# Weight sums of the first pair spread over VectorE and GpSimd, conversions moved behind the gate product, one weight quarter kept in DRAM until it is needed

## The chip, the core and the metric

The kernel runs on one core of a Trainium2 chip. A core has TensorE (PE in the profile, with its weight loads as PEld), VectorE (DVE), ScalarE (ACT), GpSimd (POOL) and SyncE (SP, which here only issues DMAs). Each engine works through its own queue of instructions in order and waits on semaphores for what the others made. The metric is the device time of one execution in microseconds, the median of several runs. The profile is one further execution, and its span is a little shorter than the timed runs.

## The reference

The program is a cross-attention between tokens and a small state, for 8 batches and 8 heads, and a feed-forward block over the joined result (cut to what matters):

```python
# x: (8, 8, 512, 64)   state: (8, 8, 32, 64)   scale = 1/8
a     = softmax(scale * x @ state.T)        # 512 x 32 for each batch and head
xread = a @ state                           # 512 x 64
a2    = softmax(scale * state @ x.T)        # 32 x 512
sread = a2 @ x                              # 32 x 64
y = concat([xread, sread], axis=2)          # 544 rows for each batch and head
y = y.transpose(0, 2, 1, 3).reshape(8 * 544, 512)
h = y @ w_in                                # 512 -> 2048
g = h * cos(h)
out = g @ w_out                             # 2048 -> 512
```

All activations are 32-bit floats. The two weight matrices, `w_in` and `w_out`, arrive as 64-bit floats; the kernel itself turns them into 32-bit ones.

## The kernel before, in words

**Tiles and steps.** The work is a list of tiles. A tile is 128 of the 2048 hidden columns of one batch: PE makes `h` for the batch's 512 tokens in PSUM (`hidden`, L490), then the gate turns it into `g` in four instructions that alternate between ACT and DVE:

- `gate`, ACT L560: rounds `h` to a whole number of turns
- `gate2`, DVE L563: subtracts, which leaves the fraction
- `gate3`, ACT L566: the sine of it, shifted, which is the cosine
- `gate4`, DVE L580: the product with `h`, written to `g_all`

One tile is one step: 16 steps for each of 8 batches, then 16 for the states. Batches are taken in pairs, 32 steps each (`PERIOD`). In the first pair (`first_pair`, steps 0 to 27, and the first four steps of the general schedule, `later_pair`, 28 to 31) two tiles of `h` are in flight, in two PSUM banks. From the second pair on, two tiles are gated in one instruction (128x1024). The main loop at the end of the program emits, step after step, the instructions of every engine in a fixed order. What comes earlier in the loop stands earlier in an engine's queue. A list for each step (`stage_at`, `sums_at`, `outer_at`, `weights_at`) says what is added in it beside the gate. The steps of attention for the next batch are put in by `plan`, as lists by engine (`go(0)` is PE, `go(1)`, `go(2)` and `go(5)` ACT, `go(3)` and `go(4)` DVE).

**Attention is folded in.** The product of states and `w_in` is made once for each batch (`products`, kept in `sw`), so that `h` needs a depth of 256 (8 heads of 32 states) in place of 512.

**The second product saves multiplications.** `out = g @ w_out` is done for a pair of batches as a two-by-two block product with 7 instead of 8 multiplications (Winograd's form): `p1` to `p7`, each with a weight block of its own, a sum or difference of the quarters `a11`, `a12`, `a21`, `a22` of `w_out`. Each of the seven is done in the same way once more inside (`Product`, 7 stages of 8 PE instructions each, L745). The sums of `g` that these need are made by DVE (`outer_sum`, L692) and POOL (`sums`, L692). From batch 2 on, three quarters of the `h` tiles are also done with 7 blocks: `seven_part` on PE (L540), `sw_sums` on POOL for the weights (L523, into `swS_all`), and `halves` on DVE for the attention side (L509, into `aS_all`). Only for batch 0 of the first pair are `p1` and `p2` done plainly, tile after tile, beside the gate (`first_product` in steps 4 to 11, `second_product` in odd steps 13 to 27, L633), with `a11` and `a12`.

**The weights are prepared in the first pair.** They are loaded raw as 18 blocks (1 MB for most), into three buffers, `raw_at`. `convert(i, parts)` turns block i into 32-bit floats: parts "1" and "2" are on ACT (L243, L246; "2" leaves its part in `low`, which is the memory of `aS_all`), "b" and "c" on DVE (L249, L252), "d" on POOL (L257), and "f" issues the load of a later block into the freed buffer. `conv_at` names the block of a step: blocks 4 to 12 in steps 0 to 8, blocks 13 to 17 in steps 11 to 15. ACT does "1" and "2" in that step; DVE and POOL do their parts in the next one, between `gate2` and `gate4`.

Then the seven weight blocks of `p1` to `p7` are made by `weight_sum` (L1092: outer sums over a whole quarter) and, for each of the seven, `inner_weights` (L671: four sums on POOL into a buffer of temporaries `TEMPS`, then eight stores to the DRAM tensor `blocks_kept`). Before, this runs in steps 16 to 25 on POOL, except for two of the outer sums, on DVE. Only `a12`'s block waits until step 50 (`last_weights`). During the pairs, `fetch_block` brings the blocks back, three stages ahead, through a ring of 4 buffers. All these DMAs are issued by SP, in order.

**Memory is tight.** `g_all` has 12 buffers of four tiles ("quads"). The list `quads_free` hands them out, oldest first, to `gate4`, to `sums`, and for temporaries; a11, a12, a21, a22 and SQ (a21+a22) occupy quads 5, 6, 7, 8 and 11 until their blocks are made. Whoever gets a quad waits for its last reader. What is freed and taken when is fixed by the order of the program's loop.

When the products start is fixed too: stage 0 of `p5` stands in step 29, and then about 1.5 stages follow in each step: `p3` from step 33, `p6` from 38, `p7` from 42, the next pair's `p1` from 47, `p4` (with `a22`) from 52, `p2` (with `a12`) from 56. The sums that a product needs are emitted from two steps ahead of its first stage.

Of the kernel before, what the change touches and what calls it, by code (L numbers as in the profile page):

```python
# [10 lines left out]
F32 = mybir.dt.float32  # L11
I32 = mybir.dt.int32
U32 = mybir.dt.uint32
ALU = mybir.AluOpType
# [8 lines left out]
def kernel(  # L23
# [55 lines left out]
    def matrix(n):  # L79
# [7 lines left out]
            for i in range(NB)]  # L87
    spare = ctx.enter_context(tc.tile_pool(name="spare", bufs=1,
                                           space=bass.MemoryType.DRAM))
    blocks_kept = spare.tile([7, 8, P, QT * P], F32)  # L90

    xT = consts.tile([P, NK, S], F32)
    x_b = consts.tile([P, NC, H, D], F32)
# [515 lines left out]
    def store(b, half, src):  # L609

        def go(ch):
            ot = osb.tile([P, S], F32, name="ot")
            nc.vector.transpose(out=ot.rearrange("p (j i) -> p j i", i=32),
                                in_=src.t[:, ch].rearrange(
                                    "p (j i) -> p j i", i=32))
            rows = out[b * T:b * T + S, :].rearrange("(j t) d -> t j d", t=32)
            src.done()

            def send():
                for q in range(P // 32):  # L620
                    c0 = HD * half + P * ch + 32 * q
                    nc.sync.dma_start(
                        out=rows[:, :, c0:c0 + 32],
                        in_=ot[32 * q:32 * q + 32].rearrange(
                            "p (j i) -> p j i", i=32))
            stores_due.append(send)
        later.extend([(now[0] + 1, lambda: go(0)), (now[0] + 2, lambda: go(1))])

# [28 lines left out]
        m = m.rearrange("p (k i) (m d) -> p m k i d", k=2, m=2)  # L659
        return m[:, 0, 0], m[:, 0, 1], m[:, 1, 0], m[:, 1, 1]  # L660

    def inner_weights(which, m, temps=TEMPS):

        m11, m12, m21, m22 = quarters(m)
        t1, t2, t3, t4 = [quad(temps)[:, n].rearrange("p (i d) -> p i d", d=P)
                          for n in range(4)]
        for o, x1, x2, op in ((t1, m21, m22, ALU.add),
                              (t2, t1, m11, ALU.subtract),
                              (t3, m11, m21, ALU.subtract),
                              (t4, m12, t2, ALU.subtract)):  # L670
            nc.gpsimd.tensor_tensor(o, x1, x2, op=op)  # L671
        for n, block in enumerate((m11, m12, t4, m22, t1, t2, t3, m21)):
            nc.sync.dma_start(
                out=blocks_kept[which, n].rearrange("p (i d) -> p i d", d=P),
                in_=block)

    stage_list = []

# [391 lines left out]
    for n in range(B // 2):  # L1070
        end = n == B // 2 - 1
        for r, engine, o, x1, x2, half in (
                ((25, 26), dve, 0, 2, 0, 0), ((27, 28), dve, 0, 2, 0, 1),
                ((31, 31), pool, 2, 3, 2, 0), ((33, 33), dve, 0, 3, 0, 0),
                ((34, 34 + (not end)), dve, 0, 3, 0, 1),
                ((35, 36), dve, 2, 3, 2, 1),
                ((38 - end,) * 2, pool, 1, 1, 0, 0),
# [7 lines left out]
                     for r in (o, x1, x2)]  # L1085
        sub(engine, o, x1, x2)

    def weight_sum(engine, o, x1, x2, op):
        n = 1 if engine is pool else 2
        for i in range(0, QT, n):  # L1090
            o_, x1_, x2_ = [quad(q)[:, i:i + n] for q in (o, x1, x2)]
            engine.tensor_tensor(o_, x1_, x2_, op=op)  # L1092

    def last_weights():
        temps = quads_free.pop(0)
        inner_weights(1, a12, temps)
        weights_at[53].append(lambda: quads_free.extend([A12, temps]))

    A11, A12, A21, A22, SQ = 5, 6, 7, 8, 11
    add_, sub_ = ALU.add, ALU.subtract  # L1100
    for at_, what in (
            (15, lambda: quads_free.append(10)),
            (16, lambda: inner_weights(2, a22)),
            (17, lambda: quads_free.append(9)),
            (17, lambda: weight_sum(pool, SQ, A21, A22, add_)),
            (18, lambda: inner_weights(3, matrix(SQ))),
            (18, lambda: weight_sum(dve, A21, A11, A21, sub_)),
            (19, lambda: inner_weights(0, a11)),
            (20, lambda: weight_sum(pool, A22, SQ, A11, sub_)),
            (21, lambda: inner_weights(5, matrix(A21))),  # L1110
            (22, lambda: inner_weights(4, matrix(A22))),
            (23, lambda: quads_free.append(A11)),
            (24, lambda: weight_sum(dve, SQ, A12, A22, sub_)),
            (25, lambda: quads_free.append(A21)),
            (25, lambda: inner_weights(6, matrix(SQ))),
            (27, lambda: quads_free.extend([A22, SQ, TEMPS])),
            (50, last_weights)):
        weights_at[at_].append(what)

    n_stages = 0  # L1120

# [17 lines left out]
    def first_pair(step, t):  # L1139
# [13 lines left out]
        else:  # L1153
# [9 lines left out]
            go(3)  # L1163
            if step == 1:
                convert(4, "bcdf")
            elif last >= 0:
                convert(last, "bcdf")
            if conv >= 0 and not todo[1]:
                convert(conv, "1")
# [2 lines left out]
        if step == 3:  # L1172
            part(0, "products_kept", 1, SIDE)
        gate4(t)
        if conv >= 0 and todo[1] and step > 0:
            convert(conv, "1")
        if step == 6:
# [1 line left out]
        go(2)  # L1179
        if conv >= 0:  # L1180
            convert(conv, "2")
        go(4)

    def later_pair(step, t, ahead):
        coming = ahead[0] if ahead and ahead[0].paired else None
# [40 lines left out]
    for step, t in enumerate(all_tiles):  # L1226
# [26 lines left out]
            outer_sum(*what)  # L1253
        for pd, k in sums_at[step]:
            pd.sums(k)
        if t.b < B - 1 and t.b > 0 and s in (12, 13):
            halves(t.b + 1, s - 12)
        if 4 <= step < 4 + NH:
            first_product(pairs[0], step - 4)
        if 13 <= step < 13 + 2 * NH and not even:  # L1260
# [46 lines left out]
```

## Time and profile before

| | us |
|---|---|
| median of 3 runs | 765.34 (764.28 to 766.12) |
| span of the profiled execution | 762.7 |
| PE busy | 721.2 |
| POOL busy | 516.9 |
| DVE busy | 490.1 |
| ACT busy | 330.9 |
| POOL L692 waiting for PE | 62.8 in 11 waits |
| POOL L692 waiting for DVE L692 | 45.5 in 13 waits |
| POOL L671 waiting for stores to `blocks_kept` | 11.6 in 3 waits |

How to read it: the busy time of an engine counts only its own instructions, so the sum over engines is far above the span. A wait is idle time of an engine just before an instruction, put down to what ended it last. A wait matters only where the engine that waits is on the chain that sets the end, or holds up one that is. PE's instructions overlap, and the time of one that stands alone is counted longer than in a dense row. Names such as L692 are lines of the kernel; a helper such as `sub` gives all its callers one line, so they are told apart by the engine, by their shapes and by the time.

### The profile page before, as it was taken

How to read it: one execution, taken by the hardware profiler on the slowest of the kernel's cores; microseconds unless marked ns; L12 is line 12 of the kernel's file. 1: busy time of each engine (PE TensorE's matmuls, PEld its weight loads, DVE VectorE, ACT ScalarE, POOL GpSimd, SP SyncE). 2: the span in 40 equal slices, each digit the busy share in tenths (PEclk: the TensorE clock that was granted, in tenths of full speed). 3: DMA queues.
4: the chain of work that ended last, by engine and by line, in shares of the span. 5: the costliest groups of instructions: out<-in, count | busy, mean ns of one | idle time of the engine just before them, and what ended most of it. 6: DMA issues, size and time to landing. Idle time of an engine off the chain costs nothing.

```text
span 762.7 us, 10471 instructions
## 1 busy us (share of the span) xinstructions
PE 721.2 (95%) x3552; PEld 507.0 (66%) x3552; DVE 490.1 (64%) x683; ACT 330.9 (43%) x538; POOL 516.9 (68%) x480
## 2 busy tenths in 40 slices
PE   8998887779999999999999999999999999999998
PEld 3443322337777876677768876687778767888886
DVE  5768786783886757686866667759746446264650
ACT  3877962633454445434363445343634432211110
POOL 2344267779799895378998952479989534799600
PEclk9999998999999999999999999999999999999999
DMA  8495359679422685477225843672224456445661
GB/s 248 166 275 173 125 118 273 223 243 188 117 86 75 139 239 144 106 140 170 76 77 113 190 109 93 134 193 84 75 69 120 111 164 156 116 144 192 180 156 40
DMA packets 210356, 111.32 MB, mean 146 GB/s; under 512 B 158272, under 2 KB 173120, under 8 KB 210304
## 3 DMA queue, kind: packets, MB, share of 16 engines
q1 hardware_dynamic: 209216, 110.14, 55.3%
q8 instruction: 28, 0.46, 0.3%
q10 hardware_dynamic: 960, 0.39, 0.2%
q14 instruction: 24, 0.20, 0.1%
q0 software_dynamic: 128, 0.13, 0.1%
HBM read 87.03 MB, written 23.59 MB: 145 GB/s over the span
## 4 chain that ended last, share of the span: by engine, by line
PE 60%; POOL 20%; DVE 5%; DMA 5%; issue 4%; ACT 3%; SPq 1%; POOLq 0%; DVEq 0%; ACTq 0%
PE o L745 31%; POOL g_all L692 13%; PE h L490 10%; PE h L540 9%; POOL g_all L671 4%; PE at L328 3%; PE at L846 2%; DMA g_all<-blocks_kept 2%; POOL swS_all L523 2%; PE at L425 1%; DMA blocks_kept<-g_all 1%; POOL sw L523 1%; DMA x_b<-in_x_dram 1%; PE o L921 1%; PE o L846 1%
## 5 line engine op out<-in xcount | busy, mean ns | idle before, releaser
L692 POOL TENSOR_TENSOR g_all<-g_all 128x512 f32<-128x512 f32 x256 | 336.4, 1345 | 108.3 <-PE o L745 62.8
L745 PE MATMUL o<-g_all 128*128 128x256 f32 x1456 | 345.2, 382 | 4.4 <-POOL g_all L692 2.4
L745 PEld LDWEIGHTS o<-g_all 128*128 128x128 f32 x1456 | 273.9, 191 | 65.3 <-issue 19.2
L563 DVE TENSOR_TENSOR q_all<-q_all,h 128x1024 f32<-128x1024 int32 (+1 forms) x88 | 85.4, 970 | 58.7 <-ACT q_all L560 58.6
L490 PE MATMUL h<-aT,sw 128*128 128x512 f32 x224 | 108.8, 610 | 12.8 <-DVE g_all L580 12.1
L566 ACT ACTIVATE q_all<-q_all,halfpi 128x1024 f32<-128x1024 f32 (+1 forms) x88 | 84.3, 958 | 61.8 <-DVE q_all L563 61.7
L580 DVE TENSOR_TENSOR g_all<-h,q_all 128x1024 f32<-128x1024 f32 (+1 forms) x88 | 85.7, 974 | 34.6 <-ACT q_all L566 32.3
L560 ACT ACTIVATE q_all<-h 128x1024 int32<-128x1024 f32 (+1 forms) x88 | 73.5, 835 | 74.3 <-DVE g_all L580 32.3
L490 PEld LDWEIGHTS h<-aT,sw 128*128 128x128 f32 x224 | 41.5, 193 | 59.8 <-issue 32.1
L549 DVE TENSOR_TENSOR h<-h,sums_all 128x256 f32<-128x256 f32 x72 | 30.9, 429 | 63.7 <-PE h L540 49.0
L692 DVE TENSOR_TENSOR g_all<-g_all 128x1024 f32<-128x1024 f32 x40 | 56.7, 1433 | 0.1
L540 PE MATMUL h<-aS_all,swS_all 128*128 128x256 f32 x144 | 45.8, 400 | 7.3 <-POOL swS_all L523 5.5
L750 ACT COPY o<-o 128x256 f32<-128x256 f32 x26 | 9.3, 357 | 88.0 <-PE o L745 88.0
L540 PE MATMUL h<-aT,sw 128*128 128x256 f32 x144 | 44.7, 392 | 2.9 <-DVE g_all L580 2.5
L671 POOL TENSOR_TENSOR g_all<-g_all 128x512 f32<-128x512 f32 x28 | 37.7, 1371 | 12.2 <-DMA blocks_kept<-g_all 11.6
L257 POOL TENSOR_TENSOR w_in<-w_in,aS_all 128x1024 int32<-128x1024 int32 (+1 forms) x10 | 19.3, 1927 | 37.6 <-DVE w_in L252 22.3
L540 PE MATMUL h<-aS_all,sw 128*128 128x256 f32 x144 | 43.5, 384 | 0.0
L540 PEld LDWEIGHTS h<-aS_all,swS_all 128*128 128x128 f32 x144 | 25.5, 191 | 26.6 <-issue 7.8
L756 ACT COPY o<-sums_all 128x256 f32<-128x256 f32 x26 | 9.8, 378 | 74.0 <-PE o L745 74.0
L603 DVE SCALAR_TENSOR_TENSOR held<-o,held 128x512 f32<-128x512 f32 x40 | 27.1, 680 | 21.3 <-PE o L745 20.8
L461 ACT COPY sw<-at 128x512 f32<-128x512 f32 x50 | 26.8, 588 | 31.3 <-PE at L328 31.3
L257 POOL TENSOR_TENSOR g_all<-g_all,aS_all 128x1024 int32<-128x1024 int32 x8 | 18.9, 2363 | 29.3 <-DVE g_all L252 22.0
(112 smaller groups left out, 869.1 us busy)
## 6 DMA issues: line engine op xcount, KB each, us to landing
g_all<-blocks_kept SPq DMA_DIRECT2D x202, 256.0 KB, 2.8
blocks_kept<-g_all SPq DMA_DIRECT2D x56, 256.0 KB, 3.0
g_all<-in_moe_w_out_dram SPq DMA_DIRECT2D x8, 1024.0 KB, 5.1
out_dram<-ot SPq DMA_DIRECT2D x128, 64.0 KB, 2.0
g_all<-in_moe_w_in_dram SPq DMA_DIRECT2D x6, 1024.0 KB, 5.9
xT<-in_x_dram SPq DMA_DIRECT2D x96, 64.0 KB, 3.0
x_b<-in_x_dram SPq DMA_DIRECT2D x24, 256.0 KB, 4.9
x_b<-in_x_dram SPq DMA_DIRECT2D x16, 128.0 KB, 4.4
```

What stands on the lines that cost most here:

```text
L257: nc.gpsimd.tensor_tensor(bits, bits, e, op=ALU.add)
L490: nc.tensor.matmul(out=t.hp, lhsT=t.lhs(i), rhs=t.rhs(i), start=(i == 0), stop=(i == t.kn - 1))
L540: nc.tensor.matmul(out=out_, lhsT=w, rhs=r, start=start, stop=True, skip_group_check=True)
L549: nc.vector.tensor_tensor(o, h2[:, LO], sums_all[:, 0], op=ALU.add)
L560: nc.scalar.activation(t.q.bitcast(I32), t.hp, func=ACTF.Copy, bias=0.25)
L563: nc.vector.tensor_tensor(t.q, t.q.bitcast(I32), t.hp, op=ALU.subtract)
L566: nc.scalar.activation(t.q, t.q, func=ACTF.Sin, bias=halfpi, scale=-TWO_PI)
L580: nc.vector.tensor_tensor(g, t.hp, t.q, op=ALU.mult)
L603: nc.vector.scalar_tensor_tensor(out=out.t[:, ch], in0=bank, scalar=TWO_PI, in1=b.t[:, ch], op0=ALU.mult, op1=ALU.add)
L671: nc.gpsimd.tensor_tensor(o, x1, x2, op=op)
L692: engine.tensor_tensor(o[:, i:i + n], x1[:, i:i + n], x2[:, i:i + n], op=ALU.subtract)
L745: nc.tensor.matmul(out=o, lhsT=ring[(self.first + k) % NB][:, i], rhs=g[:, i], start=(start and i == 0), stop=(i == QT - 1), skip_group_ch ...
```

## The change

It concerns steps 5 to 31, where the weights are converted and summed, and steps 41 to 56, where two of the weight blocks are now made.

- *Conversion.* From step 5 to 10, DVE's and POOL's parts of a block's conversion stand behind `gate4` instead of before it. From step 11 they stand at the end of the block's own step, not in the next. This is to let the gate go ahead of the conversion.
- *Sums on DVE.* Of the four outer sums, POOL keeps a21+a22. The other three are DVE's, as two halves each, in steps 18 and 19, 20 and 22, 23 and 24. Before, two of them were on DVE (steps 18 and 24, both halves together) and one on POOL.
- *Inner sums.* `a11`'s four POOL instructions are spread over steps 12 to 15. A second buffer of temporaries, the memory of `aS_all`, takes turns with `TEMPS`, so that POOL needn't wait for stores. `halves`, which writes that memory, comes a step later in batch 1.
- *Stores.* The four blocks that need no sum are stored at once, the four made by POOL in the next step.
- *a22.* Its quad is needed for SQ-a11, so it is copied to a new DRAM tensor, `kept`, in step 17, fetched back in steps 41 to 44, and its blocks are made in step 46; those of `a12` in step 51. Both are stored spread over four steps.
- *Other sums.* Half of the L692 sums of the first pair on DVE comes a step earlier (steps 26 and 27), and the first output's transposes (`store`) two steps later.

The diff, cut to its core:

```diff
+    kept = spare.tile([QT, P, S], F32)
...
-        later.extend([(now[0] + 1, lambda: go(0)), (now[0] + 2, lambda: go(1))])
+        n = now[0] + 2 * (now[0] < PERIOD - 4)
+        later.extend([(n + 1, lambda: go(0)), (n + 2, lambda: go(1))])
...
-    def inner_weights(which, m, temps=TEMPS):
+    def inner_weights(which, m, temps, pieces=range(4), at_step=None):
...
+        def send(i):
+            block = (m11, m12, m22, m21, t4, t1, t2, t3)[i]
...
+        if at_step is None:
+            for i in range(4 if 3 in pieces else 0):
+                send(i)
+                stores_due.append(lambda i=i: send(4 + i))
+        else:
+            for i in range(8):
+                weights_at[at_step + (i + 1) // 2].append(
+                    lambda i=i: send(i))
...
-                ((25, 26), dve, 0, 2, 0, 0), ((27, 28), dve, 0, 2, 0, 1),
+                ((25, 26), dve, 0, 2, 0, 0),
+                ((27 - (not n), 28 - (not n)), dve, 0, 2, 0, 1), ((31, 31), pool, 2, 3, 2, 0), ((33, 33), dve, 0, 3, 0, 0),
...
+    def late_weights(step):
+        if step == 41:
+            late_quads.append(quads_free.pop(0))
+        if step < 45:
+            move(False, late_quads[0], step - 41)
+        if step == 46:
+            late_quads.append(quads_free.pop(0))
+            inner_weights(2, matrix(late_quads[0]), quad(late_quads[1]),
+                          at_step=step)
+        elif step == 51:
+            quads_free.append(late_quads[0])
+            inner_weights(1, a12, quad(late_quads[1]), at_step=step)
...
+    temps = [quad(TEMPS), aS_all.rearrange("p n i s -> p (n i s)").rearrange(
+        "p (t s) -> p t s", s=S)]
+    for i in range(QT):
+        weights_at[12 + i].append(lambda i=i: inner_weights(
+            0, a11, temps[0], (i,)))
+        weights_at[17].append(lambda i=i: move(True, A22, i))
+    for steps, o, x1, x2, op in (
+            ((18, 19), A21, A11, A21, ALU.subtract),
+            ((20, 22), A22, SQ, A11, ALU.subtract),
+            ((23, 24), SQ, A12, A22, ALU.subtract)):
...
-            (16, lambda: inner_weights(2, a22)),
+            (16, pool_sum),
...
-            (17, lambda: weight_sum(pool, SQ, A21, A22, add_)),
-            (18, lambda: inner_weights(3, matrix(SQ))),
-            (18, lambda: weight_sum(dve, A21, A11, A21, sub_)),
-            (19, lambda: inner_weights(0, a11)),
-            (20, lambda: weight_sum(pool, A22, SQ, A11, sub_)),
-            (21, lambda: inner_weights(5, matrix(A21))),
-            (22, lambda: inner_weights(4, matrix(A22))),
+            (17, lambda: inner_weights(3, matrix(SQ), temps[1])),
+            (20, lambda: inner_weights(5, matrix(A21), temps[0])),
+            (23, lambda: inner_weights(4, matrix(A22), temps[1])),
...
-            elif last >= 0:
+            elif last >= 0 and step < 5:
                 convert(last, "bcdf")
...
         gate4(t)
+        if last >= 0 and 4 < step < 11:
+            convert(last, "bcdf")
...
+        if step > 10 and conv >= 0 and not todo[1]:
+            convert(conv, "bcdf")
         go(4)
+        if step > 10 and conv >= 0 and todo[1]:
+            convert(conv, "bcdf")
...
-        if t.b < B - 1 and t.b > 0 and s in (12, 13):
-            halves(t.b + 1, s - 12)
+        n = s - 12 - (t.b == 1)
+        if t.b < B - 1 and t.b > 0 and n in (0, 1):
+            halves(t.b + 1, n)
```

## The prediction

> **What bounds the kernel now.** I read the page first, parts 1 and 2.
>
> ```profile
> PE 721.2 (95%) x3552; PEld 507.0 (66%) x3552; DVE 490.1 (64%) x683; ACT 330.9 (43%) x538; POOL 516.9 (68%) x480
> ...
> PE   8998887779999999999999999999999999999998
> POOL 2344267779799895378998952479989534799600
> PEclk9999998999999999999999999999999999999999
> ```
>
> TensorE (PE) is busy 95%, with no spare capacity from slice 11 on (a slice is 19 us). Below 9 it stands in slices 4 to 10 (57 to 190 us): the first pair of batches. In slice 7 its granted clock dips, and GpSimd (POOL) stands at 7 to 9 just then. So the change must pay between 60 and 200 us or not at all. The windows of 20 us size it (columns: time, PE, PEld, DVE, ACT, POOL busy, clock, DMA share, GB/s):
>
> ```profile
> 100.00:120.00 20.00, 15.04 (x67) 4.89 (x65) 13.26 (x15) 7.85 (x13) 15.93 (x12) 1.00 0.52 133
> 120.00:140.00 20.00, 17.45 (x52) 5.96 (x52) 13.90 (x21) 8.50 (x13) 15.85 (x12) 0.83 0.92 253
> 140.00:160.00 20.00, 15.10 (x76) 6.66 (x76) 17.19 (x24) 10.00 (x18) 12.22 (x10) 0.91 0.67 213
> 160.00:180.00 20.00, 14.91 (x54) 9.76 (x47) 12.56 (x17) 5.61 (x12) 19.61 (x21) 0.91 0.88 220
> ...
> 240.00:260.00 20.00, 20.00 (x115) 16.23 (x114) 11.57 (x19) 6.43 (x12) 17.37 (x21) 1.00 0.54 118
> ```
>
> From 100 to 180 us PE is busy 62.5 of 80 us, and inflated: a 128x512 matmul shows 610 ns on average in the groups, while the chain has four of them in 1.73 us, 432 ns each, when they run densely. From 240 us it is 20.00 of 20. Next the timeline around the dip (start, duration, engine):
>
> ```profile
> 113.97 5.91 POOL L1092 TENSOR_TENSOR g_all<-g_all 128x512 f32<-128x512 f32 x4
> 116.50 2.27 DVE L1092 TENSOR_TENSOR g_all<-g_all 128x1024 f32<-128x1024 f32 x1 [3.87 <-POOL g_all L1092]
> 119.92 1.23 DVE L1092 TENSOR_TENSOR g_all<-g_all 128x1024 f32<-128x1024 f32 x1 [1.15 <-POOL g_all L1092]
> 121.78 0.72 ACT L566 ACTIVATE q_all<-q_all,halfpi 128x512 f32<-128x512 f32 x1 [8.39 <-DVE q_all L563]
> 122.42 3.46 PE L328 MATMUL at<-xT,st_all 64*32 64x512 f32 x8 [5.59 <-DVE xT L310]
> ...
> 170.75 0.45 POOL L523 TENSOR_TENSOR swS_all<-sw 128x128 f32<-128x128 f32 x1
> 171.25 1.22 PE L540 MATMUL h<-aS_all,swS_all 128*128 128x256 f32 x2 [4.70 <-POOL swS_all L523]
> ```
>
> POOL's sum a21+a22 (L1092) keeps VectorE (DVE) waiting 3.87 and 1.15 us; behind those DVE instructions stand the gate's subtraction (ScalarE, ACT, waits 8.39 us) and the transposes of the tokens (PE waits 5.59 us, then runs 8 matmuls in 3.46 us that take 1.06 at full clock). At 171 us PE waits 4.70 us for POOL, which had finished its weight sums only at 164.5. The chain of waits agrees: from 106.6 to 164.5 it is almost all POOL L257, L671, L1092 and stores of their results. Waits and groups:
>
> ```profile
> POOL g_all L671 <- DMA blocks_kept<-g_all: 11.6, 3, 4.0
> ...
> L692 POOL TENSOR_TENSOR g_all<-g_all 128x512 f32<-128x512 f32 x256 | 336.4, 1345 | 108.3 <-PE o L745 62.8 <-DVE g_all L692 45.5
> L692 DVE TENSOR_TENSOR g_all<-g_all 128x1024 f32<-128x1024 f32 x40 | 56.7, 1433 | 0.1
> L671 POOL TENSOR_TENSOR g_all<-g_all 128x512 f32<-128x512 f32 x28 | 37.7, 1371 | 12.2 <-DMA blocks_kept<-g_all 11.6
> ```
>
> GpSimd also waits 11.6 us for stores out of its single buffer of temporaries. POOL's 128x512 (1.345 us) and DVE's 128x1024 (1.433 us) give the prices: DVE does a sum twice as fast.
>
> **What the skill says.** "GPSIMD Engine Reference", section 4.1, names VectorE first for elementwise work and GpSimd about two times slower with two inputs; the two rows above agree (1.88 times). "SBUF — State Buffer", section "Who interferes with whom", says that the two share a port pair, and that a DVE instruction in a two-port mode, or with two inputs in SBUF, blocks whole against GpSimd's reads. The trace agrees:
>
> ```profile
> 97.98 2.36 POOL L257 TENSOR_TENSOR g_all<-g_all,aS_all 128x1024 int32<-128x1024 int32 x1 [3.03 <-DVE g_all L252]
> 99.07 1.83 DVE L249 TENSOR_SCALAR g_all<-g_all 128x1024 int32<-128x1024 int32 x1
> ```
>
> The 128x1024 shift takes 0.69 us alone and 1.83 beside POOL. "TensorE: Matmul & The Clock Gate", "What's actually happening", puts the half clock after an idle window of some 3.4 us; here half speed follows idle times of 5.59 and 4.70 us, but at 151 us one of 2.47 us too, less than the page's window.
>
> **The change, part by part.** Let D(s) be the start of the gate's first DVE instruction (L563) of step s. Before: D(9) 70.4, D(16) 102.7, D(19) 121.1, D(21) 129.0, D(23) 135.8, D(25) 148.7, D(28) 160.7, D(30) 172.0, D(31) 180.4. The order of PE and ACT instructions is unchanged; DVE, POOL and the store queue change. I laid the new DVE order out with durations from the trace: L563 0.60 from start to start, wait for ACT's sine 0.8, L580 0.60, conversion 0.69+1.15.
>
> *Conversion behind the gate product, steps 5 to 15.* It removes 1.9 us from in front of L580 but leaves the wait for the sine, 0.8 us, unfilled: ring 0.6+0.8+0.6+1.9, about 4.0 us, against ACT's own 0.48+1.05+0.63+1.05, 3.2 us, plus copies. PE doesn't profit: in steps 6 to 9 its own queue is full (50.5 to 58.4 and 59.6 to 71.0 us). My layout gives D(9) 70.8 and D(16) 103.8: 1.1 us later. But the last conversion now runs before step 16, so its L580 is at 105.1, not 106.4, and POOL ends conversions near 106.2 instead of 109.0.
>
> *Sums moved.* a11's four POOL instructions (5.1 us) go between conversions, where POOL waits 2 us each time. a22's four (5.1 us) leave this stage; A22 = SQ-A11 goes from POOL (5.0 us) to DVE (2 x 1.43 us). POOL's a21+a22 then runs at 107.5 to 113.0, not 114.0 to 119.9. The layout on DVE: L580(16) 105.1; D(17) 105.8; D(18) 108.2, its transposes around L580 until 110.8; first half of A21 to 112.6 (1.8 us beside POOL, whose tiles 0 and 1 were done at 110.2); D(19) 112.6; second half 115.2 to 116.8; D(20) 116.8, the maximum (two of 0.65 us), L580 to 119.2; first half of A22 to 120.7. The A22 halves cost DVE 2.9 us; their wait for the copies of a22 to DRAM (four stores issued near 114 to 116, 3 us each) ends near 118 to 119, as DVE arrives at 119. If it were late, everything queued behind on DVE, the gates of step 21 first, would be, and PE behind them. In the store queue, which is worked in order, those copies stand behind a11's computed blocks (POOL, 107.5) and four loads of x_b (4.0 us). D(21) 120.7; spread, shift, maximum and the second half (6.5 us with two gates' 2.0 each) give D(23) 129.1; exponentials with two table loads of 1.28 us on ACT, row sums, inverse, spread and norm, SQ's halves: D(25) 141.3.
>
> *Second buffer and raw blocks first.* The 11.6 us of waits for stores go; POOL now waits for DVE's sums instead, some 6 us twice, which nobody feels: its last weight block ends at 146.4, not 164.5.
>
> *Sums and transposes spread, halves a step later.* Same work, in other steps: a half of L692 goes from step 28 to 26, the store's transposes (0.70 us) from 28 and 29 to 30 and 31, where DVE waited for PE 1.3 to 1.9 us at a time. The transposes' outputs leave two steps later, which nobody reads. D(28) 155.1, D(30) 163.0: 9.0 us earlier than 172.0. swS then comes out of POOL by 159.5, so the 4.70 us at 171 are gone, replaced by the wait for the halves (161.5). From there on the work to the dense phase is the old one (POOL's chain of 197 to 236 us), shifted by 9.
>
> *a22 fetched back and summed at step 46, a12 at 51.* 5.1 us more on POOL where it is not idle:
>
> ```profile
> 271.79 5.09 POOL L671 TENSOR_TENSOR g_all<-g_all 128x512 f32<-128x512 f32 x4
> 289.50 9.88 POOL L692 TENSOR_TENSOR g_all<-g_all 128x512 f32<-128x512 f32 x8 [3.34 <-PE o L745]
> ```
>
> The same stretch of the next pair has no L671, and its PE is as dense; POOL ends there with 8.4 us of idle instead of 3.34. The extra 5.1 us use this up plus about 1.7 us. The nearest deadline is swS: made at 259.1 to 261.1, first read by PE at 265.3; later by 5.1, its first part is ready 0.6 us ahead. Next, a sum must wait for a buffer freed in its own step 50, and is due some 9 us later. So between 0 and 2 us; I take 0.5. Four loads and spread stores cost queue time only (0.5 us each).
>
> Sum: -9.0 + 0.5 = -8.5 us; 765.3 - 8.5 = 756.8 us.
>
> **Rivals.**
> A. *More comes out.* PE's work in steps 16 to 31, at dense rate, is about 58 us (16 tiles, 6 plain products, 5 stages at 1.73, attention 11) against 78 now. If the new DVE instructions fall into DVE's waits (24 us from 108 to 180) and the clock stays up, 15 us go: 750. For it: D(19) alone is 8.5 us early, and clock losses show three times. Against: DVE has 57 us of work there already, plus 3.
> B. *The conversions eat it.* If the unfilled 0.8 us is paid in all ten moved steps (8 us) rather than hidden under ACT, little stays: 763.5. For it: DVE is busy 17.1 of 20 us from 60 to 80. Against: ACT is busier still from 80 to 100 (17.8).
> C. *Slower.* The gain shrinks as in B, and the late sums miss deadlines: two waits of 3 us at steps 48 to 52 and a store queue in order that holds back the next weight block. 765.3 - 2 + 6 = 769. For it: the slack of 0.6 us, and buffers without reserve from step 40 to 54. Against: the dense PE in the stretch with L671.
>
> **How the numbers follow.** Forecast 0.48, A 0.20, B 0.18, C 0.14. Faster takes the forecast, A and two thirds or more of B: 0.82. Same, a sliver of B: 0.04. Slower, C: 0.14. The range runs from below A, 747 (3 us for errors of my layout), to 767, which leaves out most of C and the best of A, no more than 2 in 10.
>
> **What would show it.** Right: no DVE wait over 2 us for POOL L1092's successor lines; POOL's weight sums of this stage done near 146; the 128x512 L560 of step 30 some 9 us before 169.7; the dense phase from about 231, and a pair period near 158.8 kept. Wrong: gates of steps 6 to 16 later by more than 2 us (B); DVE waiting for a store at step 20; or PE idle on swS or on weight blocks between 240 and 290 (C).

## The result, and the profile after

The changed kernel takes 758.64 us (median of 4 runs, 757.45 to 759.70), the kernel before 765.55 beside it. The ratio is 0.9912 with a 95% interval of 0.9892 to 0.9932: faster, by 6.9 us. The forecast was 756.8 us in a range of 747 to 767. The profiled spans are 755.6 and 762.7 us.

First the page of the changed kernel, parts 1 and 2 (a slice is 18.9 us):

```profile
PE 717.8 (95%) x3552; PEld 505.1 (67%) x3552; DVE 493.6 (65%) x685; ACT 330.7 (44%) x538; POOL 514.3 (68%) x476
...
PE   8999879779999989999999999999999999999998
POOL 2343477676998985387998853579989534799600
PEclk9999999999999999999999999999999999999999
```

Counted from 0, PE's slices 3 and 6 have risen from 8 and 7 to 9, slice 5 has fallen from 8 to 7, and the clock dip is gone. Slice 14, 264 to 283 us, has fallen from 9 to 8. The windows size both (time, then PE, PEld, DVE, ACT, POOL busy, clock, DMA share, GB/s):

```profile
100.00:120.00 20.00, 17.72 (x75) 5.90 (x73) 16.57 (x19) 9.62 (x17) 17.39 (x12) 0.91 0.78 177
120.00:140.00 20.00, 16.70 (x58) 6.65 (x56) 16.70 (x24) 10.17 (x18) 13.34 (x10) 1.00 0.99 325
140.00:160.00 20.00, 14.42 (x77) 6.84 (x76) 17.40 (x22) 7.37 (x13) 12.90 (x8) 1.00 0.75 213
160.00:180.00 20.00, 18.17 (x86) 12.57 (x84) 11.88 (x18) 9.02 (x19) 17.96 (x20) 1.00 0.66 136
...
240.00:260.00 20.00, 20.00 (x114) 15.28 (x114) 12.95 (x19) 8.48 (x15) 17.40 (x20) 1.00 0.76 153
260.00:280.00 20.00, 17.93 (x107) 13.92 (x105) 10.51 (x16) 8.49 (x15) 16.49 (x20) 1.00 1.06 261
```

The last of these windows in the kernel before:

```profile
260.00:280.00 20.00, 20.00 (x104) 16.38 (x103) 13.24 (x21) 8.24 (x15) 18.34 (x21) 1.00 0.84 181
```

From 100 to 180 us PE is busy 67.0 us, before it was 62.5, and more of that at a low clock: the clock was at 0.83 and 0.91 in three of the windows before, now it is at 0.91 in one. From 260 to 280 us, where PE had been full before (20.00), it now lacks 2.07 us, and the DMA engines are at 1.06 instead of 0.84. Where the gain arises, in the timelines of POOL, DVE and PE:

```profile
110.44 4.97 POOL L1148 TENSOR_TENSOR g_all<-g_all 128x512 f32<-128x512 f32 x4
144.60 6.06 POOL L674 TENSOR_TENSOR g_all<-g_all 128x512 f32<-128x512 f32 x4 [6.70 <-DVE g_all L1105]
...
114.31 2.19 DVE L1105 TENSOR_TENSOR g_all<-g_all 128x1024 f32<-128x1024 f32 x1
123.61 1.20 DVE L1105 TENSOR_TENSOR g_all<-g_all 128x1024 f32<-128x1024 f32 x1
...
164.69 0.67 PE L541 MATMUL h<-aS_all,swS_all 128*128 128x256 f32 x2 [1.38 <-DVE aS_all L510]
```

POOL's sum a21+a22 (L1148) starts 3.5 us earlier than before, and DVE's next sum (L1105, at 114.31) no longer waits for it. POOL's last weight block starts at 144.60 and ends at 150.7, not at 164.5. PE's wait for `swS` of 4.70 us at 171 us has become one of 1.38 for `halves`.

And the new loss, in the timelines of SyncE and PE (of the DMAs, the duration is the time to issue them):

```profile
257.14 1.04 SPq L698 DMA_DIRECT2D g_all<-blocks_kept  x1
258.22 1.20 SPq L678 DMA_DIRECT2D blocks_kept<-g_all  x2
259.47 3.93 SPq L132 DMA_DIRECT2D x_b<-in_x_dram  x4
263.49 1.27 SPq L698 DMA_DIRECT2D g_all<-blocks_kept  x1
264.81 1.19 SPq L678 DMA_DIRECT2D blocks_kept<-g_all  x2
...
268.12 1.99 PE L760 MATMUL o<-g_all 128*128 128x256 f32 x8 [2.07 <-DMA g_all<-blocks_kept]
```

At 268.12 us PE has waited 2.07 us for a weight block. The trace gives 4.6 us from issue to landing for the fetch at 263.49 and names this wait as the one behind it; 263.49 + 4.6 is 268.1. This fetch stood behind two late stores (L678) and the four loads of `x_b` (L132), which took 3.93 us to issue.

**The lead, step by step.** A gate's first ACT instruction (L560 before, L561 after) marks its step. "Lead" below is how much earlier it starts than in the kernel before, less the same difference at step 7, where the change has hardly begun (at most 0.6 us, and 1.1 in one run). The gates of step 34, before and after, are an example:

```profile
195.25 1.02 ACT L560 ACTIVATE q_all<-h 128x1024 int32<-128x1024 f32 x1 [1.41 <-PE h L540]
185.98 1.02 ACT L561 ACTIVATE q_all<-h 128x1024 int32<-128x1024 f32 x1 [1.41 <-PE h L541]
```

The difference is 9.27 us, less 0.10 at step 7. From the timelines:

```
step               17    18    21    30    31    34    50    52    54   (us; minus: later than before)
changed kernel   -3.2  -1.9   5.7   6.3   8.0   9.2   9.1   6.8   7.6
```

So there are three phases: up to 3 us are lost in and just behind the conversions (a11_18 below shows by what), steps 19 to 34 bring 11, and between steps 50 and 52 2.3 us are lost again. (Before step 54 the kernel before loses 0.7 us to a wait of the same kind.)

### The profile page after: what moved, and what is told of

Read it like the earlier page. It is cut to its first block, busy times and chain, and to the rows that moved or that the text cites. A ratio compares the mean times of both kernels' runs of the same rounds, so it can differ in the third digit from the quotient of the medians.

```text
span 755.6 us, 10478 instructions
## 1 busy us (share of the span) xinstructions
PE 717.8 (95%) x3552; PEld 505.1 (67%) x3552; DVE 493.6 (65%) x685; ACT 330.7 (44%) x538; POOL 514.3 (68%) x476
## 4 chain that ended last, share of the span: by engine, by line
PE 57%; POOL 17%; issue 2%; DVE 2%; DMA 1%; ACT 1%; DVEq 0%; POOLq 0%
PE o L760 31%; POOL g_all L707 13%; PE h L491 9%; PE h L541 9%; PE at L329 2%; PE at L861 2%; POOL swS_all L524 2%; POOL sw L524 1%; PE at L426 1%; DMA g_all<-blocks_kept 1%; PE o L861 1%; DVE xT L311 1%; DVE g_all L707 0%; ACT sw L462 0%; ACT q_all L567 0%
## 5 line engine op out<-in xcount | busy, mean ns | idle before, releaser
L707 POOL TENSOR_TENSOR g_all<-g_all 128x512 f32<-128x512 f32 x256 | 337.4, 1350 | 107.9 <-PE o L760 60.7
L561 ACT ACTIVATE q_all<-h 128x1024 int32<-128x1024 f32 (+1 forms) x88 | 73.2, 832 | 66.3 <-DVE g_all L581 34.1
L491 PEld LDWEIGHTS h<-aT,sw 128*128 128x128 f32 x224 | 41.0, 191 | 59.5 <-issue 31.3
L707 DVE TENSOR_TENSOR g_all<-g_all 128x1024 f32<-128x1024 f32 x40 | 56.8, 1438 | 0.1
L258 POOL TENSOR_TENSOR g_all<-g_all,aS_all 128x1024 int32<-128x1024 int32 x8 | 18.9, 2366 | 23.8 <-DVE g_all L253 11.3
L541 PEld LDWEIGHTS h<-aT,sw 128*128 128x128 f32 x144 | 25.9, 189 | 13.0 <-DVE g_all L581 9.8
```

Source lines behind the costliest of these rows:

```text
L258: nc.gpsimd.tensor_tensor(bits, bits, e, op=ALU.add)
L491: nc.tensor.matmul(out=t.hp, lhsT=t.lhs(i), rhs=t.rhs(i), start=(i == 0), stop=(i == t.kn - 1))
L541: nc.tensor.matmul(out=out_, lhsT=w, rhs=r, start=start, stop=True, skip_group_check=True)
L561: nc.scalar.activation(t.q.bitcast(I32), t.hp, func=ACTF.Copy, bias=0.25)
L707: engine.tensor_tensor(o[:, i:i + n], x1[:, i:i + n], x2[:, i:i + n], op=ALU.subtract)
```

## The experiments

All times are medians, and the ratio is to the kernel before on the same chip (765.2 to 766.1 us). The kernel before differs by up to 0.9 us between these chips, so a difference of two medians is uncertain by as much, and the ratios are safer. Line numbers of the experiments are those of the changed kernel, but for L1105 and above, which shift by a few lines, and for conv_only, which has those of the kernel before. Leads are corrected as above; those in the expectations are not.

| run | us | ratio (95%) | lead at step 34 | PE waits near 268 us |
|---|---|---|---|---|
| changed kernel | 758.64 | 0.9912 (0.9892 to 0.9932) | 9.2 | 2.07 |
| conv_back | 758.50 | 0.9916 (0.9902 to 0.9929) | 9.2 | 2.54 |
| conv_only | 762.56 | 0.9964 (0.9952 to 0.9977) | 1.7 | none |
| xb_late | 755.24 | 0.9873 (0.9858 to 0.9888) | 9.2 | none |
| late_nosum | 758.10 | 0.9909 (0.9896 to 0.9923) | 9.2 | 2.23 |
| a11_18 | 757.07 | 0.9892 (0.9877 to 0.9906) | 11.8 | 2.16 |
| a11_18_xb | 752.45 | 0.9836 (0.9822 to 0.9850) | 11.3 | none |
| no_defer | 755.95 | 0.9880 (0.9866 to 0.9894) | 8.0 | none |
| w2_first | 759.45 | 0.9918 (0.9902 to 0.9935) | 4.2 | none |
| one_buf | 759.87 | 0.9940 (0.9921 to 0.9959) | 7.9 | 2.05 |
| a22_pool | 757.78 | 0.9888 (0.9871 to 0.9905) | 10.7 | 2.06 |
| spread_back | 762.02 | 0.9945 (0.9931 to 0.9959) | 6.7 | 2.17 |
| nodef_a11 | 754.56 | 0.9852 (0.9838 to 0.9866) | 10.3 | none |

**The late loss: xb_late and late_nosum.**

```diff
-        load_now(H if step < NF else 4)
+        if step not in range(47, 53):
+            load_now(H if step < NF else 4)
```

> The changed kernel with the four loads of x_b, which were queued at step 47 between the late stores of weight blocks, held back to step 53. My theory: the 2.1 us wait of TensorE for a weight block near 268 us comes from that block's fetch being queued behind the 3.9 us of these loads on SyncE, so it goes and the run takes 756.0 to 757.2 us (1.4 to 2.6 less than the changed kernel). Rival (the loss comes from GpSimd's late weight sums, or from the sheer bytes, which stay): 758.2 to 759 us, with a wait of over 1 us left there.

```diff
-            nc.gpsimd.tensor_tensor(o, x1, x2, op=op)
+            if at_step is None:
+                nc.gpsimd.tensor_tensor(o, x1, x2, op=op)
```

> The changed kernel with the eight late GpSimd operations (the weight sums of a22 at step 46 and of a12 at step 51) left out; their blocks are stored as they lie in the buffer, so two of the seven inner products are computed from other weights. All transfers stay. My theory: the loss near 268 us is one of the transfer queue, so nothing changes: 758.0 to 759.2 us, wait of 2 us still there. Rival (GpSimd's late sums make the second sums or the stores late): 756.8 us or less, and the wait gone.

With the loads held back the wait is gone and 3.4 us come off (3.0 by the ratios), more than expected. Without POOL's late sums the wait stays, and so does the time. So it isn't POOL but the transfer queue. SyncE and PE of xb_late:

```profile
258.11 0.43 SPq L698 DMA_DIRECT2D g_all<-blocks_kept  x1
258.59 1.20 SPq L678 DMA_DIRECT2D blocks_kept<-g_all  x2
259.89 0.58 SPq L698 DMA_DIRECT2D g_all<-blocks_kept  x1
260.52 1.20 SPq L678 DMA_DIRECT2D blocks_kept<-g_all  x2
...
265.83 1.89 PE L760 MATMUL o<-g_all 128*128 128x256 f32 x8
```

The same fetch, the second L698 here, is issued at 259.89 instead of 263.49, and PE goes on at 265.83 without a gap. The trace gives 4.0 us from its issue to landing, against 4.6. So of the 4.2 us by which the block is there earlier, 3.6 come from its place in the queue and 0.6 from a shorter time to landing.

That xb_late gains more than the wait of 2.1 us may have a second reason. In a11_18 (below) PE waits 2.16 us at the same place, and what follows runs at a lower clock. Its PE timeline:

```profile
264.06 0.59 PE L541 MATMUL h<-aS_all,swS_all 128*128 128x256 f32 x2
266.81 3.31 PE L760 MATMUL o<-g_all 128*128 128x256 f32 x8 [2.16 <-DMA g_all<-blocks_kept]
```

and its windows of 4 us (columns as above, the clock is the third number from the end):

```profile
264.00:268.00 4.00, 1.84 (x8) 1.26 (x7) 2.13 (x3) 1.50 (x3) 0.81 (x2) 0.92 1.16 320
268.00:272.00 4.00, 4.00 (x13) 3.21 (x13) 0.98 (x3) 0.00 (x0) 2.98 (x4) 0.66 1.15 277
```

The 8 matmuls take 3.31 us, against 1.99 after the wait in the changed kernel's profile, and the clock is 0.66. Between steps 50 and 52 a11_18 loses 4.1 us, conv_back 4.5, the changed kernel in its profile only 2.3. That profile was the fastest of its four runs (757.45; the others are 758.26 to 759.70). The others may have lost the clock at this place too, but they have no profile, so this isn't shown. In the profiles alone, xb_late is ahead by 2.8 us at step 70.

**The conversion: conv_back, conv_only, a11_18.** In conv_back the four new places of `convert` are undone:

```diff
-            elif last >= 0 and step < 5:
+            elif last >= 0:
                 convert(last, "bcdf")
...
-        if last >= 0 and 4 < step < 11:
-            convert(last, "bcdf")
...
-        if step > 10 and conv >= 0 and not todo[1]:
-            convert(conv, "bcdf")
...
-        if step > 10 and conv >= 0 and todo[1]:
-            convert(conv, "bcdf")
```

> The changed kernel with the conversions of the first pair put back ahead of the gate product from step 5 on; all else as changed (758.6 us). My theory: the gain comes from the weight sums, and the moved conversions only cost (the gate of step 17 came 3.1 us later than before), so undoing the move gives 755.5 to 758.5 us, with the gate of step 17 starting at 105 to 106 us instead of 108.0, and the lead over the kernel before at step 40 still 9 us or more. Rival (the conversion move is what frees VectorE, and the sums only follow it): 761 us or more, with a lead of 6 us or less at step 40.

conv_only is the kernel before with these same lines put in.

> The kernel before (765.5 us) with the moved conversions alone. My theory: no gain, 765 to 768.5 us, since the wait of VectorE for GpSimd's weight sum at step 18 stays and absorbs or lengthens what the gate lost. Rival (the move is worth something by itself): 763 us or less.

conv_back changes nothing (758.50, at the edge of what I expected; the gate of step 17 starts at 107.5, not at 105 to 106). conv_only was a clear miss: the move alone makes the kernel before 2.6 us faster (1.7 us of lead at step 34, and 0.8 more at step 54, where the kernel before has its wait). Its POOL and DVE:

```profile
103.96 2.36 POOL L257 TENSOR_TENSOR g_all<-g_all,aS_all 128x1024 int32<-128x1024 int32 x1 [1.96 <-DVE g_all L252]
111.32 5.91 POOL L1092 TENSOR_TENSOR g_all<-g_all 128x512 f32<-128x512 f32 x4
...
113.84 2.27 DVE L1092 TENSOR_TENSOR g_all<-g_all 128x1024 f32<-128x1024 f32 x1 [2.40 <-POOL g_all L1092]
```

The last conversion ends at 106.3 us. Before it was 109.0, and a21+a22 starts at 111.32 instead of 113.97. So in the kernel before the move does what it is for. In the changed kernel it ends the conversions earlier too, at 109.25 us against 111.64 in conv_back. Of that 0.9 us reach the DVE gate of step 18 (111.60 against 112.51), and the first half of A21 behind it then takes 2.19 us (at 114.31, above) against 1.20 in conv_back:

```profile
115.22 1.20 DVE L1105 TENSOR_TENSOR g_all<-g_all 128x1024 f32<-128x1024 f32 x1
116.34 0.68 DVE L564 TENSOR_TENSOR q_all<-q_all,h 128x512 f32<-128x512 int32 x1
```

The DVE gate of step 19 starts at 116.34 there and at 116.42 in the changed kernel, so nothing is left. Both halves start beside POOL's sum a21+a22; in conv_back that sum took longer instead (5.95 us against 4.97). What decides which of the two engines is held up stays open.

In both kernels `a11`'s sums stand between the conversions and make them longer. In the changed one (POOL's L674, DVE's conversion part "c", L253):

```profile
98.67 1.74 POOL L674 TENSOR_TENSOR g_all<-g_all 128x512 f32<-128x512 f32 x1
103.96 1.71 POOL L674 TENSOR_TENSOR g_all<-g_all 128x512 f32<-128x512 f32 x1
...
99.31 2.18 DVE L253 SCALAR_TENSOR_TENSOR g_all<-g_all 128x1024 int32<-128x1024 int32 x1
104.58 2.17 DVE L253 SCALAR_TENSOR_TENSOR g_all<-g_all 128x1024 int32<-128x1024 int32 x1
```

"c" takes 2.18 us beside such a sum, against 1.22 alone, and POOL's next conversion waits for "c". The ring, from one of POOL's conversions to the next, is 5.27 us long instead of 4.33 in conv_only. a11_18 takes the four sums out, to step 18 (the buffers of the later blocks change turns):

```diff
-        weights_at[12 + i].append(lambda i=i: inner_weights(
-            0, a11, temps[0], (i,)))
...
+            (18, lambda: inner_weights(0, a11, temps[0])),
-            (20, lambda: inner_weights(5, matrix(A21), temps[0])),
-            (23, lambda: inner_weights(4, matrix(A22), temps[1])),
+            (20, lambda: inner_weights(5, matrix(A21), temps[1])),
+            (23, lambda: inner_weights(4, matrix(A22), temps[0])),
```

> The changed kernel with the four GpSimd sums of a11 taken from between the conversions (steps 12 to 15) and done together at step 18, after the weight sums of SQ. In the runs so far the last conversion ends on GpSimd at 106.3 us with the moved conversions alone, but at 109.25 with a11's sums between them. My theory: each of these sums runs into VectorE's next conversion operation (2.2 us instead of 1.2), so that without them the conversions end near 106.3, the gate of step 17 starts near 105 us, VectorE reaches step 21 some 2 to 3 us earlier, and 1.5 to 3 us of it arrive at step 34: 755.5 to 757.2 us. Rival (from step 18 on VectorE waits for GpSimd's sum a21+a22 or the first dense stages are set by another wait, as the equal lead of both placements of the conversions suggests): 758 to 759.5 us, with the conversions earlier and the lead at step 34 unchanged at 9.3 us.

```profile
99.56 1.22 DVE L253 SCALAR_TENSOR_TENSOR g_all<-g_all 128x1024 int32<-128x1024 int32 x1
103.89 1.22 DVE L253 SCALAR_TENSOR_TENSOR g_all<-g_all 128x1024 int32<-128x1024 int32 x1
...
105.26 2.36 POOL L258 TENSOR_TENSOR g_all<-g_all,aS_all 128x1024 int32<-128x1024 int32 x1 [1.95 <-DVE g_all L253]
```

"c" is back at 1.22 us, the conversions end at 107.6 (106.5 with the shift of this run at step 7 taken off), and the lead at step 34 grows from 9.2 to 11.8 us. Only 1.6 of these 2.6 us reach the end, since the late wait, with its lower clock, is dearer here. With the `x_b` loads held back too (this diff and that of xb_late together) they arrive:

> The same and the x_b loads held back to step 53. My theory: both gains add, 752.0 to 754.0 us, below the 755.2 us of the loads alone. Rival: 754.8 to 755.8 us, that is the loads alone.

752.45 us: both gains add. This is the fastest of all, 1.6% below the kernel before and 6.2 us below the changed one (5.8 by the ratios). Whether the moved conversions still pay once `a11`'s sums are out of the way was not tried.

**The deferral of a22: no_defer, w2_first, nodef_a11.** no_defer makes a22's blocks at step 16, behind a21+a22, and has no copy in DRAM:

```diff
-        weights_at[17].append(lambda i=i: move(True, A22, i))
...
-            (17, lambda: inner_weights(3, matrix(SQ), temps[1])),
-            (20, lambda: inner_weights(5, matrix(A21), temps[0])),
-            (23, lambda: inner_weights(4, matrix(A22), temps[1])),
+            (16, lambda: inner_weights(2, a22, temps[1])),
+            (18, lambda: inner_weights(3, matrix(SQ), temps[0])),
+            (20, lambda: inner_weights(5, matrix(A21), temps[1])),
+            (23, lambda: inner_weights(4, matrix(A22), temps[0])),
...
-    for step in (41, 42, 43, 44, 46, 51, 56):
+    for step in (51, 56):
```

> The changed kernel without the deferral of a22: its four sums are done on GpSimd at step 16 after a21+a22, its blocks are stored then, and the four stores to and four loads from the kept copy, the four late sums and the eight late stores fall away; the x_b loads stay at step 47. My theory: with the late stores gone from the queue the wait near 268 us goes although the x_b loads stand where they stood (gain of 2 to 4 us there), and the early stage loses 0 to 5 us since GpSimd's weight sums then end near 156 us and not 150.7: 755 to 760 us, with the lead at step 34 between 5 and 9.3 us. Rival A (the x_b loads alone delay the block): the wait of 2 us or more stays. Rival B (deferring a22 is where most of the 9 us comes from): lead at step 34 under 4 us and over 761 us.

It is 2.7 us faster than the changed kernel (2.4 by the ratios): it loses 1.2 us of the early lead and doesn't have the late wait. SyncE:

```profile
257.38 0.45 SPq L698 DMA_DIRECT2D g_all<-blocks_kept  x1
257.88 4.35 SPq L132 DMA_DIRECT2D x_b<-in_x_dram  x4
262.33 2.06 SPq L698 DMA_DIRECT2D g_all<-blocks_kept  x3
```

The `x_b` loads (L132) stand where they stood, and no wait follows. So neither these loads nor `a22`'s late stores make the wait alone; it takes both. w2_first then turns only the order of a22's sums and a21+a22 round:

```diff
+            (16, lambda: inner_weights(2, a22, temps[1])),
             (16, pool_sum),
-            (16, lambda: inner_weights(2, a22, temps[1])),
```

> The run without the deferral of a22, with one thing turned round: GpSimd does a22's four weight sums ahead of the sum a21+a22, as the kernel before did, and not behind it. My theory: what the deferral was good for is the place of a21+a22 in GpSimd's queue. It then runs 5.1 us later, some 116 to 121 us, VectorE's first half of A21 waits 3 to 5 us for it with the transposes and the gate of step 20 behind it, and the lead at step 34 falls from 7.3 to 3 to 5 us: 758.0 to 760.5 us, against 755.95 without the turn. Rival (the sums of a22 are hidden either way, the gain comes from the finer halves on VectorE): 755.5 to 756.5 us, no wait of VectorE for GpSimd over 1 us.

```profile
115.40 5.91 POOL L1139 TENSOR_TENSOR g_all<-g_all 128x512 f32<-128x512 f32 x4
...
117.91 2.27 DVE L1105 TENSOR_TENSOR g_all<-g_all 128x1024 f32<-128x1024 f32 x1 [3.61 <-POOL g_all L1139]
```

As expected: DVE's half of A21 waits 3.61 us for POOL again, and the lead falls by 3.7 us against no_defer. That is the largest single piece found. nodef_a11 is no_defer with `a11`'s sums at step 19 as well, all of them behind the last conversion:

```diff
-        weights_at[12 + i].append(lambda i=i: inner_weights(
-            0, a11, temps[0], (i,)))
...
-            (16, lambda: inner_weights(2, a22, temps[1])),
-            (18, lambda: inner_weights(3, matrix(SQ), temps[0])),
-            (20, lambda: inner_weights(5, matrix(A21), temps[1])),
+            (16, lambda: inner_weights(2, a22, temps[0])),
+            (18, lambda: inner_weights(3, matrix(SQ), temps[1])),
+            (19, lambda: inner_weights(0, a11, temps[0])),
+            (21, lambda: inner_weights(5, matrix(A21), temps[1])),
```

> The run without the deferral of a22, with the sums of a11 also taken from between the conversions and done at step 19, so that GpSimd has all its sums behind the last conversion, in the order a21+a22, a22, SQ, a11, A21, A22, SQ, with no copy in DRAM and no late sums but a12's. My theory: the conversions end near 106.3 us again, a21+a22 3 us earlier, and GpSimd's two idle stretches (4.4 and 6.7 us) take up the moved sums: lead at step 34 of 9.5 to 11.5 us, no wait for a weight block near 268 us: 752.3 to 754.5 us, at least as good as 752.45 within 2 us with less code. Rival (stores and memory traffic of 120 to 145 us, where the transfer engines were at 0.99 already, hold up GpSimd's buffers and the first fetched blocks): 755.5 us or more.

754.56 us, just above what I expected, lead 10.3, no late wait. It is slower than a11_18_xb by 2.1 us in the medians and 1.2 by the ratios, whose intervals overlap, but it needs no copy in DRAM.

**The other parts: one_buf, a22_pool, spread_back.**

```diff
-    temps = [quad(TEMPS), aS_all.rearrange("p n i s -> p (n i s)").rearrange(
-        "p (t s) -> p t s", s=S)]
+    temps = [quad(TEMPS), quad(TEMPS)]
```

> The changed kernel with one buffer of temporaries for the weight sums instead of two. My theory: GpSimd then waits for stores again before three of the sums, but VectorE's own sums set the pace of the stage (GpSimd stands idle 4.4 and 6.7 us waiting for them), so no more than 0 to 3 us are lost: 758.5 to 761.5 us. Rival (the second buffer and the stores' order bring most of the 9 us): 763 us or more, with GpSimd's waits for stores back at over 10 us in all.

```profile
128.06 6.07 POOL L674 TENSOR_TENSOR g_all<-g_all 128x512 f32<-128x512 f32 x4 [5.70 <-DMA blocks_kept<-g_all]
146.13 6.92 POOL L674 TENSOR_TENSOR g_all<-g_all 128x512 f32<-128x512 f32 x4 [3.16 <-DMA blocks_kept<-g_all]
153.01 4.70 POOL L707 TENSOR_TENSOR g_all<-g_all 128x512 f32<-128x512 f32 x3
```

POOL waits for stores again (11.8 us in three waits), and its next sum of `g` (L707) starts at 153.01 instead of 150.62. The lead loses 1.3 us.

```diff
-            ((20, 22), A22, SQ, A11, ALU.subtract),
...
+            (22, lambda: pool_sum((A22, SQ, A11), ALU.subtract)),
```

> The changed kernel with A22 = SQ - A11 back on GpSimd (four operations of 1.24 us at step 22) in place of the two halves on VectorE. My theory: GpSimd stands idle 4.4 us just there and VectorE is the engine that sets the pace of steps 20 to 24, so this costs nothing and may give back up to the 2.4 us of the two halves: 757 to 759 us, lead at step 34 9.3 to 11 us. Rival (putting this sum on VectorE is a main part of the 9 us): lead under 7 us and 760.5 us or more.

The lead grows by 1.5 us: the third sum on DVE costs, and doesn't bring anything here. The intervals of the two times overlap, so this rests on the lead.

spread_back undoes three lines:

```diff
-        n = now[0] + 2 * (now[0] < PERIOD - 4)
+        n = now[0]
...
-                ((27 - (not n), 28 - (not n)), dve, 0, 2, 0, 1), ((31, 31), pool, 2, 3, 2, 0), ((33, 33), dve, 0, 3, 0, 0),
+                ((27, 28), dve, 0, 2, 0, 1), ((31, 31), pool, 2, 3, 2, 0), ((33, 33), dve, 0, 3, 0, 0),
...
-        n = s - 12 - (t.b == 1)
+        n = s - 12
```

> The changed kernel with the transposes of the store, the half of the difference of rows at step 27 and the halves of the tokens put back into the steps where they stood before. My theory: they fill the same steps 23 to 30 of VectorE but stand before gates again, 1 to 3 us lost: lead at step 34 6.3 to 8.3 us, 759.5 to 761.5 us. Rival (these moves are without weight, since VectorE waits for TensorE there anyway): 758.2 to 759.2 us, lead 9 us or more.

The lead loses 2.5 us, the time 3.4 (2.5 by the ratios), a little more than expected. Which of the three moves counts was not tried.

## Why the prediction was right, and where it wasn't

The time was 1.8 us above the forecast, well within the range, and the main case was the one that came. But its two terms hide errors, two of which cancel by luck.

- *Conversion behind the gate product.* Forecast: POOL done near 106.2, D(16) at 103.8. Measured: 109.25 and 106.67. What failed is the term "a11's four POOL instructions (5.1 us) go between conversions, where POOL waits 2 us each time": this was counted as free. In a11_18_xb, without it, POOL is done at 106.3 and D(16) is 103.68. "SBUF — State Buffer" in the Trainium skill, section "Who interferes with whom", says that a DVE instruction with two inputs in SBUF contends with a GpSimd instruction that reads SBUF, and this case bears it out (2.18 against 1.22 us). But I applied it only to the A21 halves and not to a conversion that closes a ring. (The ring itself, worked out at about 4.0 us, is 4.33 without these sums.)
- *Sums moved.* DVE no longer waits for POOL, as said. The layout's later times were 112.6, 120.7, 129.1, 141.3 for D(19), D(21), D(23), D(25). They came 3.1 to 4.0 us later (116.42, 124.74, 132.66, 144.44), 2.4 to 3.0 us of it carried from the conversion: in a11_18_xb they are 113.53, 121.77, 130.25 and 142.07, within 1.2 us. The runs agree that the order on POOL counts most (w2_first, 3.7 us). That A22 moves from POOL to DVE is a cost, as worked out, but of 1.5 us of lead and not of 2.9.
- *Second buffer and raw blocks first.* The stores' waits went, as forecast, and no gain of its own was put on that. The trace still puts one wait of 4.41 us, before the sum at 132.82, down to a store; but that sum needs DVE's second half of A22, which ended at 132.75, so it could hardly have started earlier. one_buf shows 1.3 us, which arise at the end of POOL's chain (L707 2.4 us later). POOL's last weight block ended at 150.7 and not at 146.4, for it waits for DVE's later SQ. The raw blocks first were not tried alone.
- *Sums and transposes spread.* D(28) and D(30) were forecast at 155.1 and 163.0 and came at 158.62 and 165.87, so 6.1 us earlier than before and not 9.0. Yet the lead at step 34 is 9.2. The step "shifted by 9 from there on" took the kernel before as it stood at step 30; but that kernel loses another 3 us by step 34, behind the wait of 4.70 us. Its PE there:

```profile
172.26 3.02 PE L745 MATMUL o<-g_all 128*128 128x256 f32 x8
183.81 1.97 PE L745 MATMUL o<-g_all 128*128 128x256 f32 x8 [0.94 <-DMA g_all<-blocks_kept]
```

and PE of the changed kernel at the same place in the program as the first of these:

```profile
165.19 1.89 PE L760 MATMUL o<-g_all 128*128 128x256 f32 x8
```

8 matmuls take 3.02 us before and 1.89 after, the two just ahead of them 1.22 and 0.67, and the 0.94 us for a weight block at 183.81 is gone too. Together this is 2.6 of the 3 us. They made up for the 3 us lost in the conversions: that -9.0 came out was luck, two errors of one size.
- *Readings of the profile.* Two of them were wrong, but no term of the sum rests on them. In the prediction's counting from 1, PE stands below 9 in slices 4 to 9 (57 to 172 us), not 4 to 10. And the 8 matmuls that took 3.46 us at 122.42 were not slowed by the clock alone: each took 1.06 us against 0.60 at 115.8, and the second four started only at 123.9, behind the second transpose on DVE (L310, done at 123.84).
- *a22 fetched back.* Forecast 0.5 us, within 0 to 2, with `swS` as the near deadline. PE never waited for `swS` between 240 and 290 us. What failed is "four loads and spread stores cost queue time only (0.5 us each)": in an ordered queue this time adds up in front of a block with a deadline. It cost 2.3 us in the profile, and 3.0 to 3.4 by the times of xb_late. The rival "slower" had this mechanism, "a store queue in order that holds back the next weight block".

In sum -9.2 and +2.3 in the profile, where the forecast had -9.0 and +0.5. Of the signs named ahead, it came true that DVE has no wait over 2 us for POOL's sum, and none for a store at step 20. POOL's end (150.7) and step 30 (6.4 us earlier, not 9) were off. From step 34 to 50 the lead is 9.1 us, and 7.1 us of it are still there at 440 us and in the spans, so the later pairs kept their period. Two signs of rivals showed: gates 15 and 16 some 2.0 and 2.3 us later (B), and PE idle on a weight block between 240 and 290 us (C). The runs say that the gain is made up of several pieces (each taken away by itself: order on POOL 3.7, spread 2.5, second buffer 1.3, deferral itself 1.2; the first was measured from no_defer, and they needn't add up), and that the deferral costs more late than it brings early. How much of the 9.2 the halves of A21 in two steps bring by themselves wasn't tried.

## What to carry to other kernels

When an instruction is put into an idle gap of an engine, ask whether the gap belongs to a ring: on GpSimd beside a two-input VectorE operation, 1.3 us of "free" work made each turn 0.94 us longer. When DMAs are deferred or spread over steps, look at what stands in the same ordered queue between the last of them and the next transfer with a deadline; moving four loads without a near deadline behind it was worth 3.0 to 3.4 us. And a forecast that comes out right should still be compared time by time with its layout: here two errors of 3 us stood against each other.

## What the runs showed of the hardware that was not expected

- TensorE's clock after a short wait doesn't follow from the length of the wait alone. After waits of 2.05 to 2.23 us for a weight block (one_buf, a22_pool, the changed kernel, spread_back, late_nosum) the next 8 matmuls took 1.99 us each time. After 2.16 us in a11_18 they took 3.31 us, with the clock at 0.66 in a window of 4 us, and after 2.54 us in conv_back 3.01. In the changed kernel a wait of only 1.82 us was followed by a slow stretch:

```profile
98.68 1.98 PE L491 MATMUL h<-aT,sw 128*128 128x512 f32 x4 [1.96 <-DVE g_all L581]
103.62 3.36 PE L491 MATMUL h<-aT,sw 128*128 128x512 f32 x4 [1.82 <-DVE g_all L581]
```

The clock was 0.52 from 104 to 106 us. "TensorE: Matmul & The Clock Gate" in the Trainium skill, section "What's actually happening", puts the half clock after an idle window of some 3.4 us. These runs show it after shorter waits, and the measurement decides: the wait of some 2 us before step 52 cost between 2.3 and 4.5 us here. What else decides is not shown.
